# A hand-written task order on one core: all tasks in a new order, the first pair's operands loaded in another order, the four pieces of w_in issued together

## The chip, the core and the metric

The kernel runs on one core of a Trainium2 chip. The metric is the device time of one execution in microseconds, the median of several runs. The engines are named as in the profile: PE (matrix products; PEld is its weight load), DVE, ACT and POOL (vector work, activation functions, general work), SP (issues DMA transfers). Sixteen DMA engines move the data; transfers issued by SP go through the queue q1, those issued by POOL through q0.

## What is computed

A gated linear recurrence over the sequence feeds an MLP with a SiLU, token by token:

```python
B, H, S, D = 4, 8, 768, 48           # d_model = H * D = 384, d_ff = 2048
f = 1.0 / (1.0 + np.exp(-f_logit))
for t in range(S):
    state = f[:, :, t, :, None] * state + np.einsum('bhd,bhe->bhde', k[:, :, t], v[:, :, t])
    y[:, :, t] = np.einsum('bhd,bhde->bhe', q[:, :, t], state)
x = y.transpose(0, 2, 1, 3).reshape(B * S, H * D)     # 3072 tokens of 384
h = x @ w_in                                           # 384 -> 2048
return ((h * (1.0 / (1.0 + np.exp(-h)))) @ w_out).astype(np.float32)
```

Inputs and output are float32 in HBM; the products run in bfloat16.

## The kernel before

The sequence of each of the four batches is cut into six chunks of 128 tokens. Two chunks form a pair, and `PAIRS` lists twelve of them: pairs 0 to 3 (form T) are chunks 0 and 1 of one batch, whose tokens alternate over the partitions, so that one load of 384 KB has runs of 384 bytes; pairs 4 to 11 (form N) are the same chunk of two batches, with runs of 192 bytes. A pair goes through these tasks, each a word `kind.pair.half` in the text `PLAN`:

- `f`, `k`, `q`, `v`: loads of the pair's inputs (line 228), nearly all issued by SP.
- `E`, `L` (lines 234, 238, 241): exp(-f) and its logarithm ln(1 + .) on ACT, into `lf`. `cs` (lines 305 to 315): PE sums the logarithms along the chunk with triangular matrices (`triu`, `tincl`, `tstrict`); small products with `ones` or `halves` give the chunk's total decay.
- `ia`, `a` (line 317): exp(c) and exp(-c) of that sum c on ACT; `al` (lines 256, 319): the total decay.
- `ki`, `qg` (line 322): k times exp(c) and q times exp(-c), on DVE or POOL, into `qk`. `vb`: v cast to bfloat16 (line 182 on ACT, 184 on DVE and POOL).
- `tq`, `qkc` (lines 329, 184): `qk` transposed on PE and copied out of PSUM; or `qkD` (line 337): transposed by a DMA that SP issues.
- `sc` (lines 346, 350): scores k times q; `at` (line 354): the scores times a mask. `y`, `yi` (lines 263, 362, 366): scores times v, and q times the state of the chunk before. `d` (lines 275, 383): k times v, the chunk's share of the state; `sd`, `su` (lines 387, 393): the new state.
- `yc`, `yT`, `xc` or `yD`: y cast, transposed on PE and copied into `xT`, or transposed by a DMA.
- `mi.P.j` (line 249): six products of the MLP's first matrix, two 128-wide column blocks of h for all 256 tokens of a pair; `si` (line 254): SiLU on ACT into `hT`; `mo.P.i.n` (line 286): four products of the second matrix for one chunk; `oc`, `so`: the result copied from PSUM and stored.
- `wi.n`, `wo.n` (lines 207, 210): a quarter of w_in or w_out, read as float32 and written to SBUF as bfloat16 by a DMA that POOL issues. Piece n of w_in holds the columns of mi.P.2n and mi.P.2n+1.
- `idle.w.n` (line 436): n matrix products of w columns whose result nobody reads.

A word such as `wi.1:G:` or `qg.1.1:V:0` also names the engine (S for SP, A, V, G for POOL, P for PE) and the buffer of the class, numbered in `SLOTS`, that the task takes. The whole order is thus written out by hand or by a search outside the kernel: each engine works through its own tasks in the order of `PLAN`, strictly one after the other, and waits by semaphores for what a task reads and for the buffer that it takes. A load that takes a buffer waits, with all of SP's later work behind it, until the former content was read. `LAST` cuts the last output tile in two. Where ACT goes from SiLU to exponentials or back it loads a table (line 485); this happens 17 times in this order and in the new one.

Before the plan the kernel issues the first four loads, builds the triangular matrices, masks and the identity on POOL and DVE and clears some buffers.

## Time and profile before

| | us |
|---|---|
| median of 3 runs | 177.82 (177.65 to 178.28) |
| the profiled execution | 178.21 |
| its span, first to last instruction | 176.4 |
| PE busy | 169.9 (96%) |
| ACT busy | 130.1 (74%) |
| DVE busy | 82.2 (47%) |
| POOL busy | 61.6 (35%) |

The profiled execution's own time is 1.8 us longer than its span. Busy PE time counts matmuls from issue to modelled end, and they overlap: 576 products of 256 columns at a mean of 272 ns are busy for 69.2 us, since one is started about every 109 ns. A timeline row such as `1.37 4.45 PE ... x10` gives the start, the time from there to the end of the last one, and the count. The granted clock of PE was 1.00 throughout.

### The profile page before, as it was taken

What the parts mean: (1) busy time and instruction counts of PE and PEld (TensorE: products, weight loads), DVE (VectorE), ACT (ScalarE), POOL (GpSimd) and SP (SyncE); (2) the same over time, 40 slices, a digit from 0 to 9 for tenths busy, and PEclk for the clock granted to TensorE, in tenths of its full rate; (3) what the DMA queues carried; (4) which work ended last, traced back from release to release, by engine and by line L of the source; (5) the groups of instructions that cost most, each with busy time, mean ns of one, the idle gap of its engine ahead of it and who ended that gap; (6) DMA issues with size and microseconds to landing.
All of it is one profiled execution on the core that took longest, in us unless ns stands there. A gap on an engine that the chain in (4) does not pass through costs nothing.

```text
span 176.4 us, 4754 instructions
## 1 busy us (share of the span) xinstructions
PE 169.9 (96%) x1927; PEld 125.4 (71%) x1930; DVE 82.2 (47%) x166; ACT 130.1 (74%) x239; POOL 61.6 (35%) x104
## 2 busy tenths in 40 slices
PE   6988999999999999999999999999999999999992
PEld 2446688666886788766787686686697676786872
DVE  7189770047795784124777155035770152520101
ACT  3967578952999989999489687997699575191630
POOL 6059394002383348400646323400434880000000
PEclk9999999999999999999999999999999999999999
DMA  5999999989999999996598797899996999323202
GB/s 147 323 325 264 208 232 198 187 156 250 207 189 214 222 202 198 184 201 140 103 231 165 148 227 153 212 151 209 223 187 147 221 139 289 71 52 127 89 4 89
DMA packets 110677, 32.12 MB, mean 182 GB/s; under 512 B 104096, under 2 KB 110528, under 8 KB 110656
## 3 DMA queue, kind: packets, MB, share of 16 engines
...
q0 software_dynamic: 3936, 3.74, 11.9%
...
q8 instruction: 15, 0.25, 0.6%
...
## 4 chain that ended last, share of the span: by engine, by line
PE 72%; ACT 11%; DVE 5%; DMA 5%; issue 2%; SPq 2%; POOL 1%; DVEq 0%; POOLq 0%
PE pb L286 32%; PE pb L249 26%; DMA k<-in_k_dram 3%; ACT x L317 3%; ACT hT L254 3%; DVE qk L322 2%; PE pb L350 2%; ACT L485 2%; DMA f<-in_f_logit_dram 2%; PE pb L362 2%; PE pb L366 2%; PE pb L346 1%; PE pb L312 1%; DVE atm L354 1%; PE pb L374 1%
## 5 line engine op out<-in xcount | busy, mean ns | idle before, releaser
L249 PE MATMUL pb<-xT,w_in_sb 128*128 128x256 bf16 x576 | 69.2, 272 | 0.3 <-ACT hT L254 0.2
L286 PE MATMUL pb<-w_out_sb,hT 128*128 128x384 bf16 (+2 forms) x400 | 68.6, 320 | 0.3 <-DVE yb L184 0.3
L249 PEld LDWEIGHTS <-w_in_sb 128*128 128x128 bf16 x576 | 54.8, 98 | 9.1 <-issue 0.9
L254 ACT ACTIVATE hT<-pb 128x512 bf16<-128x512 f32 x96 | 50.5, 611 | 11.1 <-PE pb L249 10.9
L286 PEld LDWEIGHTS <-hT 128*128 128x128 bf16 x400 | 37.2, 98 | 20.8 <-issue 0.4
L393 POOL TENSOR_TENSOR st<-sd,al 48x192 bf16<-48x192 f32 x40 | 21.4, 535 | 58.5 <-PE pb L362 33.2
L317 ACT ACTIVATE x<-pb 128x384 f32<-128x384 f32 x48 | 21.1, 499 | 5.8 <-PE pb L305 3.3
L354 DVE TENSOR_TENSOR atm<-pb,triu 128x512 bf16<-128x512 f32 x32 | 20.1, 684 | 11.2 <-PE pb L350 6.6
L485 ACT ACT_TABLE_LOAD x17 | 21.8, 1283 | 0.3
L184 DVE COPY ob<-pb 128x384 f32<-128x384 f32 (+1 forms) x11 | 5.7, 528 | 26.3 <-PE pb L286 26.3
L322 POOL TENSOR_TENSOR qk<-k,x 128x384 bf16<-128x384 f32 x11 | 12.0, 1102 | 6.6 <-ACT x L317 2.2
L387 DVE TENSOR_TENSOR sd<-pb,st 128x384 f32<-128x384 f32 x16 | 8.8, 552 | 11.6 <-PE pb L383 10.1
L322 POOL TENSOR_TENSOR qk<-q,x 128x384 bf16<-128x384 f32 x11 | 11.1, 1012 | 8.7 <-DMA q<-in_q_dram 6.1
L234 ACT ACTIVATE e<-f 128x768 f32<-128x768 f32 x12 | 10.1, 839 | 4.4 <-DMA f<-in_f_logit_dram 4.4
L182 ACT COPY ob<-pb 128x384 f32<-128x384 f32 (+1 forms) x14 | 6.6, 474 | 7.6 <-PE pb L286 7.1
L322 DVE TENSOR_TENSOR qk<-q,x 128x384 bf16<-128x384 f32 x13 | 8.0, 633 | 7.7 <-ACT x L317 7.6
L354 DVE TENSOR_TENSOR atm<-pb,mask 128x512 bf16<-128x512 f32 x16 | 10.2, 684 | 2.1 <-PE pb L346 1.0
L436 PE MATMUL pb<-zero,triu 128*128 128x512 bf16 (+1 forms) x26 | 9.4, 465 | 1.4 <-POOL triu masks.py:66 1.4
L322 DVE TENSOR_TENSOR qk<-k,x 128x384 bf16<-128x384 f32 x13 | 9.1, 712 | 2.4 <-DMA k<-in_k_dram 2.1
L184 DVE CAST yb<-pb 128x384 bf16<-128x384 f32 x14 | 7.6, 554 | 5.1 <-PE pb L366 2.6
L184 DVE COPY qkTT<-pb 128x1024 bf16<-128x1024 bf16 x7 | 4.6, 682 | 10.8 <-PE pb L329 10.8
L184 POOL CAST vb<-v 128x384 bf16<-128x384 f32 x12 | 6.4, 541 | 8.8 <-DMA v<-in_v_dram 7.1
...
## 6 DMA issues: line engine op xcount, KB each, us to landing
f<-in_f_logit_dram SPq DMA_DIRECT2D x11, 384.0 KB, 5.5
k<-in_k_dram SPq DMA_DIRECT2D x10, 384.0 KB, 5.6
q<-in_q_dram SPq DMA_DIRECT2D x10, 384.0 KB, 5.2
v<-in_v_dram SPq DMA_DIRECT2D x10, 384.0 KB, 4.9
...
w_in_sb<-in_moe_w_in_dram POOLq DMA_DIRECT2D x4, 384.0 KB, 8.7
w_out_sb<-in_moe_w_out_dram POOLq DMA_DIRECT2D x4, 384.0 KB, 9.7
...
```

The lines of the kernel that those rows point to most:

```text
L184: ENG[eng].tensor_copy(dst, src)
L234: return nc.scalar.activation(e, at("f", P)[:, j * w:(j + 1) * w], AF.Exp, scale=-1.0)
L249: nc.tensor.matmul(h[:, i, cols], w_in_sb[:, kk, n * 128:(n + 1) * 128], at("xT", P)[:, kk, cols], start=(kk == 0), stop=(kk == KT - 1))
L254: return nc.scalar.activation(at("hT", P)[:, 2 * j:2 * j + 2, :], at("h", P, j).rearrange("p (n c) -> p n c", n=2), AF.Silu)
L286: nc.tensor.matmul(at("o" + key, P, i)[:, 0:cols.stop - cols.start], at("hT", P)[:, n, i * C:(i + 1) * C], w_out_sb[:, n, cols], start=(n ...
L317: nc.scalar.activation(at(kind, P, i).rearrange("p h d -> p (h d)"), at("cs", P, i)[:, 0:HD], AF.Exp, scale=1.0 if kind == "ia" else -1.0)
L322: ENG[eng].tensor_mul(at("qk", P, i)[:, j, :, 0:D], heads("qk"[j], P, i), at("ia" if j else "a", P, i))
L354: ENG[eng].tensor_mul(at("atm", P, i)[:, r], at(f"s{r}", P, i).rearrange("p (n c) -> p n c", c=C), mask[:, None, :].to_broadcast([C, NP, C]))
L387: nc.vector.tensor_add(at("sd", P, i), d_ps, prev_state(P, i))
L393: nc.gpsimd.tensor_mul(at("st", P, i)[lo:lo + D, :, r * D:(r + 1) * D], at("sd", P, i)[lo:lo + D, :, r * D:(r + 1) * D], al_of(P, i)[lo:lo ...
L436: nc.tensor.matmul(buf["pb", int(got)][:, 0:rest[0]], triu, zero[:, 0:rest[0]], start=True, stop=True, skip_group_check=True)
L485: nc.scalar.preload_act_table_set(turns[n])
```

## The change

`PLAN` is replaced as a whole: 867 words in place of 846. In counts, the tasks are the same but for these: the dummy products are 17 of 512 columns and 8 of 256, before 26 and 3; the small products of `cs` are a task of their own, `on`; the second transposed tile of pair 6 becomes one on PE (`tq.6.0`, `qkc.6.0`) in place of `qkD.6.0`; eleven `su` go from POOL to DVE, and some `vb`, `oc`, `yc`, `xc` and `qg` change engines; one store goes from SP to POOL. The buffers f, k, q and v become one class `inp` of 24, and exp(-f) is written over f, so the class e goes. Only the first two loads are issued ahead of the preparations; the making of the matrices and the identity is in the plan (`mk.0`, `mk.1`, `mk.2` on POOL, `mv` on DVE). The dummy products take their weights from `zero`, before from `triu`.

At the start, SP's order is f.1, f.0, v.1, k.1, q.1, f.2, k.0, q.0, v.0, q.2, k.2, v.2; before it was f.1, f.0, k.1, q.1, v.1, f.2, k.0, q.0, v.0, q.2, k.2, v.2. ACT takes ia.1.0 and ia.1.1 ahead of a.1.1 and a.1.0, before the other way round; DVE takes ki.1.0 and ki.1.1 ahead of qg.1.1 and qg.1.0. POOL's first tasks are mk.0, mk.1, vb.1.0, vb.1.1, mk.2, wi.1, wi.3, wi.0, wi.2, ki.0.1, qg.0.1, su.1.0, wo.0, vb.0.1, wo.1, wo.2, wo.3; before they were vb.1.0, wi.1, su.1.0, wi.3, ki.0.1, wi.0, vb.0.1, wi.2, su.0.0, wo.0, su.0.1, wo.1, qg.2.1, wo.2, wo.3. PE's order around the first MLP products is now y.1, yi.1.1, sc.0.0, sc.0.1, yT.1.0, yT.1.1, idle, mi.1.2, mi.1.3, d.0, y.0, mi.1.6, idle, yi.0.1, mi.1.7.

The core of the diff, with the first and last words of both plans:

```diff
-LAST = {(11, 0): (("", slice(0, 256)), ("2", slice(256, 384)))}
+LAST = {(11, 1): (("", slice(0, 256)), ("2", slice(256, 384)))}
-SLOTS = dict(f=4, k=6, q=6, v=6, e=2, lf=3, x=5, qk=5, vb=7, qkT=4, qkTT=2, atm=4, yb=3, xT=4, hT=4, sd=2, al=6, ob=6, pb=8, st0=1, st1=1, st2=1, st3=1)
+SLOTS = dict(inp=24, lf=3, x=5, qk=5, vb=7, qkT=4, qkTT=2, atm=4, yb=3, xT=4, hT=4, sd=2, al=6, ob=6, pb=8, st0=1, st1=1, st2=1, st3=1)
...
-f.1.0:S:0 f.1.1:A: E.1.0:A:0 L.1.0:A:0 idle.512.10::0 cs.1.1:P:0 f.0.0:S:1 E.0.0:A:1 k.1.0:S:0 L.0.0:A:1 idle.512.1::1 cs.1.0:P:1
-q.1.0:S:0 idle.512.2::2 cs.0.0:P:2 idle.256.1::3 cs.0.1:P:3 a.1.1:A:0 qg.1.1:V:0 a.1.0:A:1 ia.1.1:A:2 ki.1.1:V: idle.512.1::4 tq.1.1:P:4 ia.1.0:A:3
-ki.1.0:V:1 v.1.0:S:0 f.2.0:S:0 qg.1.0:V: idle.512.3::5 tq.1.0:P:1 vb.1.1:V:0 vb.1.0:G:1 d.1:P:5,6 qkc.1.1:V:0 qkc.1.0:V: idle.512.1::7 idle.256.1::7
-sc.1.0:P:1,4 at.1.0.0:V:0 ia.0.0:A:0 k.0.0:S:1 ki.0.0:V:0 at.1.0.1:V: idle.512.2::7 idle.256.1::7 sc.1.1:P:7,1 at.1.1.0:V:1 at.1.1.1:V: a.0.1:A:2
-ia.0.1:A:3 sd.1.0:A:0 wi.1:G: al.1:A:0 E.2.0:A:1 L.2.0:A:1 q.0.0:S:1 a.0.0:A:1 qg.0.0:V: idle.512.1::5 cs.2.0:P:0 cs.2.1:P:5 al.2:A:1 ia.2.1:A:0
-su.1.0:G:0 ia.2.0:A:4 al.0:A:2 a.2.0:A:1 qg.0.1:V:1 idle.512.2::2 y.1:P:1,7 tq.0.0:P:4 v.0.0:S:1 yc.1.0:V:0 a.2.1:A:2 qkc.0.0:A:1 sd.1.1:V:0 wi.3:G:
-ki.0.1:G: tq.0.1:P:3 qkc.0.1:V: yT.1.0:P:1 yi.1.1:P: yc.1.1:A:0 wi.0:G: idle.512.2::2 sc.0.1:P:3,4 vb.0.1:G:0 at.0.1.0:V:0 yT.1.1:P:7 xc.1.0:A:0
-sc.0.0:P:6,5 at.0.0.1:V:1 at.0.0.0:V: vb.0.0:A:1 wi.2:G: idle.512.1::2 d.0:P:3,1 xc.1.1:A: sd.0.0:A:1 su.0.0:G:0 mi.1.2:P:7 mi.1.3:P:3 at.0.1.1:V:
...
+f.1.0:S:0 f.1.1:A: E.1.0:A: L.1.0:A:0 mk.0:G: mk.1:G: mv.0:V: idle.512.10::0 cs.1.1:P:0 idle.256.1::1 cs.1.0:P:1 f.0.0:S:1 E.0.0:A: L.0.0:A:1
+idle.256.1::2 on.1:P: cs.0.1:P:2 cs.0.0:P:3 on.0:P: v.1.0:S:2 k.1.0:S:3 ia.1.0:A:0 ki.1.0:V:0 vb.1.0:G:0 ia.1.1:A:1 ki.1.1:V:1 a.1.1:A:2 a.1.0:A:3
+ia.0.1:A:0 vb.1.1:G:1 idle.512.1::4 idle.256.1::4 d.1:P:4,5 q.1.0:S:4 qg.1.1:V: mk.2:G: idle.256.1::6 tq.1.1:P:1 qg.1.0:V: qkc.1.1:V:0 tq.1.0:P:6
+qkc.1.0:V: idle.512.3::7 sc.1.1:P:6,1 a.0.0:A:1 a.0.1:A:2 ia.0.0:A:4 f.2.0:S:5 E.2.0:A: al.1:A:0 al.0:A:1 L.2.0:A:1 sc.1.0:P:2,0 cs.2.0:P:3 cs.2.1:P:7
+on.2:P: k.0.0:S:0 q.0.0:S:1 v.0.0:S:2 ki.0.0:V:0 wi.1:G: a.2.1:A:4 at.1.1.0:V:0 qg.0.0:V: wi.3:G: at.1.0.0:V:1 idle.256.1::6 tq.0.0:P:6 at.1.1.1:V:
+at.1.0.1:V: wi.0:G: wi.2:G: sd.1.0:A:0 ki.0.1:G:1 ia.2.0:A:1 qkc.0.0:A:1 ia.2.1:A:0 qg.0.1:G: idle.512.1::2 idle.256.1::2 tq.0.1:P:4 su.1.0:G:0
+idle.512.1::2 y.1:P:0,1 a.2.0:A:2 yi.1.1:P: yc.1.1:A:0 wo.0:G: qkc.0.1:V: sc.0.0:P:4,6 sc.0.1:P:3,2 vb.0.1:G:0 yc.1.0:V:1 at.0.0.0:V:0 yT.1.0:P:0
+xc.1.0:A:0 yT.1.1:P:1 xc.1.1:V: idle.512.1::4 idle.256.1::4 mi.1.2:P:1 mi.1.3:P:0 al.2:A:2 vb.0.0:A:1 d.0:P:7,4 at.0.1.1:V:1 at.0.1.0:V: at.0.0.1:V:
+y.0:P:6,3 sd.0.0:A:0 mi.1.6:P:2 su.0.0:V:0 sd.0.1:V:1 idle.256.1::7 yi.0.1:P: yc.0.0:A:0 sd.1.1:V:0 mi.1.7:P:6 q.2.0:S:4 yc.0.1:A:1 yT.0.0:P:4
+xc.0.0:V:1 k.2.0:S:3 si.1.3:A:0 su.0.1:V:0 wo.1:G: yT.0.1:P:3 mi.1.0:P:5 mi.1.1:P:4 si.1.2:A: xc.0.1:V: mi.0.2:P:3 mi.0.6:P:1 mi.0.3:P:0 mi.0.5:P:7
...
+mi.5.4:P:5 si.3.0:A: mo.3.0.0:P:6 si.3.7:A: si.3.5:A: si.3.3:A: mo.3.1.0:P:7 mo.3.1.1:P: mi.5.5:P:2 mo.3.1.2:P: tq.6.0:P:1 mo.3.1.3:P: oc.3.1:V:2
+mo.3.0.1:P: mo.3.0.2:P: vb.4.0:V:1 so.0.1:S: mi.5.7:P:7 qkc.6.0:V:1 k.4.0:S: si.5.1:A:0 si.5.4:A: ia.4.0:A:4 E.7.0:A: L.7.0:A:1 qkD.4.1:S:0 a.4.0:A:0
...
+so.8.1:G: so.10.0:S: si.11.1:A:0 mi.11.0:P:4 si.11.0:A: mi.11.3:P:0 mi.11.2:P:5 mi.11.5:P:4 si.11.2:A: mi.11.7:P:1 so.6.1:S: si.11.3:A: mo.11.0.0:P:5
+mo.11.0.1:P: si.11.5:A: mo.11.1.0:P:4,2 mo.11.1.1:P: si.11.4:A: mo.11.0.2:P: si.11.7:A: si.11.6:A: mo.11.0.3:P: oc.11.0:V:3 mo.11.1.2.0:P:
+mo.11.1.2.1:P: so.11.0:S: oc.11.1.0:A:1 so.11.1.0:A: oc.11.1.1:V:4 so.11.1.1:S:
...
-        if kind in ("wi", "wo"):
-            n, parts = rest[0], count[kind]
-            if kind == "wi":
-                w = d_ff // parts
-                nc.gpsimd.dma_start(out=w_in_sb[:, :, n * w:(n + 1) * w], in_=w_in_src[:, :, n * w:(n + 1) * w])
-            else:
-                w = NT // parts
-                nc.gpsimd.dma_start(out=w_out_sb[:, n * w:(n + 1) * w, :], in_=w_out_src[:, n * w:(n + 1) * w, :])
+        if kind == "wi":
+            cols = slice(512 * rest[0], 512 * (rest[0] + 1))
+            return nc.gpsimd.dma_start(out=w_in_sb[:, :, cols], in_=w_in_src[:, :, cols])
+        if kind == "wo":
+            rows = slice(4 * rest[0], 4 * (rest[0] + 1))
+            return nc.gpsimd.dma_start(out=w_out_sb[:, rows, :], in_=w_out_src[:, rows, :])
+        if kind == "mk":
+            if rest[0] == 2:
+                return make_identity(nc, ident)
+            return make_upper_triangular(nc, tstrict if rest[0] else triu, 1.0, diag=not rest[0])
+        if kind == "mv":
+            nc.vector.tensor_copy(tincl, triu)
+            for t in (tincl, tstrict):
+                nc.vector.memset(t[0:HC, HC:C], 0.0)
+            for r in range(2):
+                half = slice(r * HC, (r + 1) * HC)
+                for j in range(2):
+                    for t in range(2):
+                        nc.vector.tensor_copy(masks[j][half, t * HC:(t + 1) * HC], (tincl if j <= t else tstrict)[half, half])
...
-            e = at("e", P)[:, j * w:(j + 1) * w]
+            e = at("f", P)[:, j * w:(j + 1) * w]
             if kind == "E":
-                return nc.scalar.activation(e, at("f", P)[:, j * w:(j + 1) * w], AF.Exp, scale=-1.0)
+                return nc.scalar.activation(e, e, AF.Exp, scale=-1.0)
...
+        if kind == "on" and T:
+            lf, cs = at("lf", P), at("cs", P, 1)
+            for p in range(NP):
+                for j in range(2):
+                    nc.tensor.matmul(cs[:, HD + 2 * p:HD + 2 * p + 2], lf[:, j, 2 * p:2 * p + 2, :], halves,
+                                     start=False, stop=(j == 1), skip_group_check=True)
+            return
...
-                if i == 1:
-                    for p in range(NP):
-                        for j in range(2):
-                            nc.tensor.matmul(cs[:, HD + 2 * p:HD + 2 * p + 2], lf[:, j, 2 * p:2 * p + 2, :], halves,
-                                             start=False, stop=(j == 1), skip_group_check=True)
             else:
                 nc.tensor.matmul(main, triu, lf[:, i, :, 0:D], start=True, stop=True, skip_group_check=True)
-                if not last:
-                    for p in range(NP):
-                        nc.tensor.matmul(cs[:, HD + p:HD + p + 1], lf[:, i, 2 * p:2 * p + 2, :], ones, start=False, stop=True, skip_group_check=True)
+        elif kind == "on":
+            lf, cs = at("lf", P), at("cs", P, i)
+            for p in range(NP):
+                nc.tensor.matmul(cs[:, HD + p:HD + p + 1], lf[:, i, 2 * p:2 * p + 2, :], ones, start=False, stop=True, skip_group_check=True)
...
-                nc.gpsimd.tensor_mul(at("st", P, i)[lo:lo + D, :, r * D:(r + 1) * D], at("sd", P, i)[lo:lo + D, :, r * D:(r + 1) * D],
+                ENG[eng].tensor_mul(at("st", P, i)[lo:lo + D, :, r * D:(r + 1) * D], at("sd", P, i)[lo:lo + D, :, r * D:(r + 1) * D],
...
-                nc.tensor.matmul(buf["pb", int(got)][:, 0:rest[0]], triu, zero[:, 0:rest[0]], start=True, stop=True, skip_group_check=True)
+                nc.tensor.matmul(buf["pb", int(got)][:, 0:rest[0]], zero[:, 0:C], zero[:, 0:rest[0]], start=True, stop=True, skip_group_check=True)
...
-        loads = [t for t in plan if t[0] in SRC][:4]
-        for t in loads:
+        first = [t for t in plan if t[0] in SRC][:2]
+        first = [t for t in first if t[2] == "A" or t is first[0]]
+        for t in first:
             run(*t)
         nc.scalar.preload_act_table_set(TABLES["exp"])
-        make_upper_triangular(nc, triu, 1.0, diag=True)
         nc.vector.memset(zero, 0.0)
         nc.vector.memset(ones, 1.0)
         if two:
-            nc.gpsimd.memset(tincl, 0.0)
-            nc.gpsimd.memset(tstrict, 0.0)
-            for r in range(2):
-                half = slice(r * HC, (r + 1) * HC)
-                make_upper_triangular(nc, tincl[half, half], 1.0, diag=True)
-                make_upper_triangular(nc, tstrict[half, half], 1.0, diag=False)
             nc.vector.memset(halves, 0.0)
             for r in range(2):
                 nc.vector.memset(halves[r * HC:(r + 1) * HC, r:r + 1], 1.0)
         for cls in ("lf", "qk"):
             for s in range(SLOTS[cls]):
                 nc.vector.memset(buf[cls, s][:, :, :, D:64], 0.0)
-        make_identity(nc, ident)
         for b in range(B):
             nc.vector.memset(buf[f"st{b}", 0], 0.0)
-        if two:
-            for r in range(2):
-                half = slice(r * HC, (r + 1) * HC)
-                for j in range(2):
-                    for t in range(2):
-                        nc.vector.tensor_copy(masks[j][half, t * HC:(t + 1) * HC], (tincl if j <= t else tstrict)[half, half])
         for n, t in enumerate(plan):
             if n in turns:
                 nc.scalar.preload_act_table_set(turns[n])
-            if t not in loads:
+            if t not in first:
                 run(*t)
```

165 lines of the change are left out of this document (87 added, 78 removed).

## The prediction

> **What bounds the kernel now.** I read the page first: shares by engine, the forty slices and the costliest groups.
>
> ```profile
> span 176.4 us, 4754 instructions
> PE 169.9 (96%) x1927; PEld 125.4 (71%) x1930; DVE 82.2 (47%) x166; ACT 130.1 (74%) x239; POOL 61.6 (35%) x104
> PE   6988999999999999999999999999999999999992
> PEclk9999999999999999999999999999999999999999
> DMA  5999999989999999996598797899996999323202
> L249 PE MATMUL pb<-xT,w_in_sb 128*128 128x256 bf16 x576 | 69.2, 272 | 0.3 <-ACT hT L254 0.2
> L286 PE MATMUL pb<-w_out_sb,hT 128*128 128x384 bf16 (+2 forms) x400 | 68.6, 320 | 0.3 <-DVE yb L184 0.3
> L322 DVE TENSOR_TENSOR qk<-k,x 128x384 bf16<-128x384 f32 x13 | 9.1, 712 | 2.4 <-DMA k<-in_k_dram 2.1
> L322 DVE TENSOR_TENSOR qk<-q,x 128x384 bf16<-128x384 f32 x13 | 8.0, 633 | 7.7 <-ACT x L317 7.6
> ```
>
> TensorE is busy 96% of the span, and the two groups of the expert product wait only 0.3 us each. A new order can therefore win almost nothing in the long middle, but it can lose there. What is left is the start, where PE runs dummy matmuls while pairs 1 and 0 go through the recurrence. In the same slices the DMA row stands at 9: the loads are a second resource that is full. The chain of waits gives the start in order of time (start, duration, what).
>
> ```profile
> 7.54 1.15 ACT x L317 x3
> 8.71 1.34 DVE qk L322 x2
> 11.64 0.43 PE pb L436 x2
> 13.76 1.85 DVE atm L354 x3
> 17.41 0.68 DVE qkTT L184
> 18.14 0.42 PE pb L346 x16
> 19.50 0.45 PE pb L275 x16
> 19.94 1.42 PE pb L249 x12
> 21.36 0.51 PE pb L263 x32
> 36.20 0.89 PE pb L329 x16
> 168.72 4.59 PE pb L286 x40
> ```
>
> Up to 19.9 us the chain hops between ACT, DVE and PE; the first expert matmuls come at 19.94, y.0 ends at 21.87, and from there the chain is almost all PE up to 173.3. So my landmark is the end of y.0: what stands behind it is a row of PE work that only its own length sets. All times below are on the profiled execution (178.21 us, of which 176.4 is the span); the median of the three runs is 177.82, 0.39 less, and I take that off at the end.
>
> **The compute path of the new start.** f of pair 1, both exponentials and logarithms stand where they stood, so ACT comes to exp(c) at 7.54. New: ia.1.0 first, then ia.1.1, a.1.1, a.1.0. Three of them took 1.15, so ki.1.0 starts at 7.95, if k is there. For the loads I need five of SP's issues (k.1, q.1, q.0, v.0 and k.2), and from the DMA view, in the same order, their time from issue to landing, the last number of each row.
>
> ```profile
> 1.79 0.58 SPq L228 DMA_DIRECT2D k<-in_k_dram  x1
> 2.42 1.74 SPq L228 DMA_DIRECT2D q<-in_q_dram  x1
> 7.78 1.15 SPq L228 DMA_DIRECT2D q<-in_q_dram  x1
> 8.97 1.11 SPq L228 DMA_DIRECT2D v<-in_v_dram  x1
> 11.50 1.15 SPq L228 DMA_DIRECT2D k<-in_k_dram  x1
> ...
> k<-in_k_dram SPq DMA_DIRECT2D x1, 384.0 KB, 4.8
> q<-in_q_dram SPq DMA_DIRECT2D x1, 384.0 KB, 5.4
> q<-in_q_dram SPq DMA_DIRECT2D x1, 384.0 KB, 4.9
> v<-in_v_dram SPq DMA_DIRECT2D x1, 384.0 KB, 4.9
> k<-in_k_dram SPq DMA_DIRECT2D x1, 384.0 KB, 12.1
> ```
>
> SP's new order is f.1, f.0, v.1, k.1, q.1, f.2, k.0, q.0, v.0. v.1 takes k.1's place and lands at 1.79 + 4.8 = 6.6; k.1 takes q.1's and lands at 2.42 + 5.4 = 7.8, just ahead of its use at 7.95; q.1 takes v.1's, 9.0 (POOL's row below starts on it at 9.09). The places of q.0 (7.78 + 4.9 = 12.7) and v.0 (8.97 + 4.9 = 13.9) are unchanged.
>
> DVE then sets the pace: two ki 1.34, to 9.3; two qg of 0.63, to 10.55 (q has landed); two copies of 0.68, to 11.9 (the transposes, 0.89 for two tiles, lie between); ki.0.0 0.71, to 12.6; one mask product and qg.0.0, 0.68 + 0.63, to 13.9; three mask products 1.85, to 15.8. So y.1 can start at 15.8, against 15.67 before: the new order of q and k alone wins nothing there, because the old path had the same DVE work ahead of y.1. The gain comes behind it. qkc.0.1 is next on DVE, 16.5, and lets the scores of pair 0 start, against 18.14; yc.1.0 0.55, one mask product 0.68 and xc.1.1 0.36 bring mi.1.2 to 18.1, against 19.94; three more mask products 1.85 bring y.0 to 20.0 and its end to 20.5, against 21.87. That is 1.4 us won if no load is late. Of that I take 0.1 for the idle.256 (half of the 0.43 / 2 of a 512 one) that now stands behind y.0.
>
> Edits with one answer. The dummy matmuls are fewer (17 of 512 and 8 of 256, before 26 and 3), but they stand in waits, and the path above doesn't pass through them. tincl, the masks and ident move into the plan (mv, mk): POOL's mk.2 stands behind vb.1.1 and before the w_in pieces, and is needed only by the transposes at 9.9. E in place and one class of input buffers add no wait at the start: k.0, q.0 and v.0 take buffers that L.1, L.0 and vb.1.1 have left before SP comes to them. Eleven su move from POOL to DVE, which is 47% busy. qkD.6.0 becomes eight PE transposes: 0.89 / 2 = **+0.45 us** on PE, the resource that bounds the rest. The tail, one 384-wide and two cut products with their stores, keeps its form: nothing.
>
> **The w_in pieces.** This is where I expect the loss. Three views: POOL's timeline, and the packets that the two DMA queues started in 9.6 to 12.9, 15.6 to 17.2 (one row each) and 20 to 24 us (both rows).
>
> ```profile
> 3.34 0.21 POOL masks.py:197 MEMSET ident<- 128x128 bf16 x1
> 3.62 0.29 POOL masks.py:199 TENSOR_SCALAR_AFFINE_SELECT ident<-ident 128x128 bf16<-128x128 bf16 x1
> 9.09 0.55 POOL L184 CAST vb<-v 128x384 bf16<-128x384 f32 x1 [5.18 <-DMA v<-in_v_dram]
> 9.58 0.91 POOL L207 DMA_DIRECT2D w_in_sb<-in_moe_w_in_dram  x1
> 13.35 0.81 POOL L207 DMA_DIRECT2D w_in_sb<-in_moe_w_in_dram  x1
> ...
> q1 hardware_dynamic: 2837, 1.07, 117.1%
> q0 software_dynamic: 4, 0.00, 0.8%
> q0 software_dynamic: 589, 0.58, 86.0%
> q1 hardware_dynamic: 596, 0.23, 32.5%
> ```
>
> Before, w_in.1 was issued at 9.58, and until 12.9 only loads moved: 2837 packets in 3.3 us, 860 per us, 1.2 us for a load of 1024 packets (384 KB by 384 B). The second piece, issued at 13.35, had moved next to nothing by 17.2. So a piece starts 3.4 to 3.9 us after its issue. Once both queues move, they start the same number of packets, 589 and 596 in 4 us: a load gets 149 packets per us, a sixth of its rate. Before, v.0 was through (13.9) when the first piece came to speed, and the later pieces were spread by POOL's work between them.
>
> Now POOL has v.1 at 6.6, two casts of 0.55 and the identity's 0.21 + 0.29 to do, and issues the four pieces from 8.2 on in a row, 0.8 to 0.9 each. They flow from 11.6 to 12.1 on, without a break. q.0's last packets (it lands at 12.7, its data ends about 0.4 earlier, at 12.3) are touched little. v.0's 1024 packets come after that, at 149 per us: 6.9 us, to 19.2, landing 19.6. That is the low end. The high end is k.2 of before: issued at 11.50, with 12.1 to landing, 23.6; it had the queue at full rate in 15.6 to 17.2 and still landed 6.4 us after w_in.3 began, since a load has landed only with its last packet. v.0 has no such head start: the 1.6 us at full rate were worth more than a whole load, which at 149 packets per us would have taken 6.9. So the 6.4 us from 12.1, 18.5, are too short, and k.2's landing itself, 23.6, is too long, as it stood behind q.2; I set the high end at 22.2. I take **20.9**, the middle. Behind it: ACT's or POOL's cast 0.55, d.0 0.45, y.0 0.51, end 22.4 against 21.87, +0.55 us. PE can't pass d.0: the queue has mi.1.2 and mi.1.3 ahead of it (1.42, done by 19.6) and everything else behind; on ACT, sd.0.0, yc.0.0 and the first silu stand behind vb.0.0, on POOL the last three w_out pieces behind vb.0.1.
>
> Sum: 0.55 + 0.1 + 0.45 = +1.1 us. For the middle I add 0.3: the 0.3 us rows leave less than 1 us to win, and the longest such wait that I find in the chain,
>
> ```profile
> 106.06 0.32 issue
> ```
>
> 0.3 us after a row of transposes and a k load on SP, is what one misjudged landing costs; an order searched anew makes its own. 178.21 + 1.4 = 179.6; less 0.39: **179.2 us**.
>
> Weighed against the Trainium skill, "DMA: Bandwidth & Descriptors", Queues, rings and completion order: an engine goes round between the queues it has work for at packet granularity. That speaks against issuing the pieces in a row, and the trace's 589 against 596 bears it out. By that rule alone v.0 lands at my low end, 19.6, and the result would be 177.9.
>
> **Rivals.**
> *A, v.0 is in time.* If the pieces flow later or the loads keep their rate until v.0 is through, d.0 doesn't wait: -1.3 + 0.45 = -0.85 on the profile, **177.0**. For it: POOL must make descriptors for four pieces at once, which before it never did, and the second piece of before took 3.9 us, not 3.4. It decides from a landing before about 19.0. Against it: equal packets from 20 to 24.
> *B, my forecast*, v.0 between 19.6 and 22.
> *C, worse sharing.* q.0's tail is caught too and v.0 lands as late as k.2 did, 23.6: y.0 ends at 25.1, +3.2, with 0.55 **181.6**. PE would then stand still over 4 us. By "TensorE: Matmul & The Clock Gate", Part 1, an idle window of about 3.4 us halves the clock; no run here shows it, and it would add some 1.7 as an estimate from that page.
> *D, the middle goes wrong*: several landings on SP's queue are misjudged; four stalls of 0.3 above mine, **180.4**.
> *E, the pieces flow at once.* Then from 9.2 on f.2's end and k.0 crawl at 149 packets per us while the 4 x 384 w packets of 1 KB pass (10.4 us), k.0 lands near 20, q.0 at 21.3, y.1 starts at 23.8 instead of 15.8, y.0 ends at 28.5 instead of 20.5: +6.6, with 0.55 **185.0**. The rows above speak against it (3.4 us). In the skill's "DMA: Bandwidth & Descriptors", Latency and other measured facts, the first byte of a GpSimd transfer comes after about 1 us.
>
> **How the numbers follow.** Chances: A 0.25, B 0.45, C 0.14, D 0.13, E 0.03. B is likeliest, so 179.2; its own range is 177.9 to 180.4. Leaving out the best part of A, the end of C and E, the range is 176.8 to 182.0. Of this kernel, 0.3% is 0.53 us, about what a measurement can tell. Faster by more than that needs most of A (0.8 of it) and a little of B with a better middle: 0.25. Within: the rest of A, the low end of B (v.0 near 19.6 gives +0.1): 0.14. Slower: 0.61.
>
> **What would show it.** Right: v.0's time to landing over 10 us where it was 4.9; packets of both queues in equal number from about 12.5 to 20; a gap on PE before d.0 (L275's new line) released by vb, after mi.1.3; w_in.1 issued at 8.2; y.1 at about 15.8 and the first expert matmul about 18, both ahead of or level with before. Wrong: v.0 landing by 18 with y.0 done at 20.5 (A), mask products or copies of DVE as what PE waits for at d.0, stalls of PE over 0.5 us behind 25 us (D), or a first w packet before 11 us (E).

## The result: 189.17 us in place of 177.73, and the profile after

The changed kernel takes 189.17 us (median of 6 runs, 187.54 to 190.39), the kernel before 177.73 on the same chip (177.60 to 178.28): a ratio of 1.063, 95% interval 1.058 to 1.069. "Slower" was right; 179.2 was not, and the range ended at 182.0. The profiled execution is the quickest of the six, 187.54 with a span of 185.8, so the traces differ by 9.4 us and the medians by 11.4; what the other five runs lose beyond it no trace shows, but their granted clock is lower, 0.979 to 0.982 against 0.989. Here and below a median counts all runs, and a ratio leaves out those over 1.5% above the fastest of the same kernel.

The page of the changed kernel, rows as in the prediction (L266 and L310 are now the lines of mi and mo, the MLP's products, which the prediction calls expert matmuls):

```profile
span 185.8 us, 4770 instructions
PE 170.6 (92%) x1932; PEld 127.2 (68%) x1934; DVE 92.4 (50%) x192; ACT 130.3 (70%) x236; POOL 52.4 (28%) x79
PE   7683899999987999999996999999999999999993
PEclk9999799999999999999999999999999999999999
L266 PE MATMUL pb<-xT,w_in_sb 128*128 128x256 bf16 x576 | 69.8, 272 | 2.6 <-DVE xT L182 1.7
L310 PE MATMUL pb<-w_out_sb,hT 128*128 128x384 bf16 (+2 forms) x400 | 68.2, 320 | 0.0
```

PE is nearly as busy as before (170.6 us against 169.9): of the 9.4 us, 8.7 are standing still. The row by slices shows where: a hole in the fourth slice (14 to 19 us), a lower clock in the fifth, and dents in the 12th, 13th and 22nd.

**The start.** The chain of waits (start, length, what), then y.0 itself from PE's timeline:

```profile
8.00 8.30 DMA inp<-in_q_dram
16.39 0.57 DVE qk L347
17.01 0.62 PE pb L354 x8
22.59 1.47 PE pb L266 x12
24.06 0.49 PE pb L299 x16
...
24.34 0.56 PE L287 MATMUL pb<-vb,atm 64*128 64x48 bf16 x32
```

q.0, issued at 8.00, landed at 16.30 and not at 12.7. DVE waited for it, PE for DVE; y.0 ends at 24.90 against 21.87, **3.0 us late**. POOL's timeline, the DMA view of 12 to 16 us and v.0's rows show why:

```profile
8.23 3.21 POOL L211 DMA_DIRECT2D w_in_sb<-in_moe_w_in_dram  x4
...
q0 software_dynamic: 563, 0.56, 84.4%
q1 hardware_dynamic: 595, 0.22, 32.2%
...
9.18 1.06 SPq L245 DMA_DIRECT2D inp<-in_v_dram  x1
inp<-in_v_dram SPq DMA_DIRECT2D x3, 384.0 KB, 13.7
```

The row of four was issued from 8.23, as predicted, and from 12 to 16 us both queues started about the same number of packets, 595 of the loads in 4 us (149 packets per us, as predicted). v.0 landed at 9.18 + 13.7 = 22.9. The granted clock of PE, by stretches of the changed kernel (the column behind POOL's):

```profile
17.00:19.00 2.00, 1.99 (x18) 1.59 (x19) 1.75 (x3) 1.81 (x4) 1.93 (x4) 0.67 1.21 206
19.00:21.00 2.00, 1.64 (x51) 1.28 (x53) 1.25 (x2) 0.58 (x3) 0.60 (x1) 0.50 1.20 206
21.00:22.00 1.00, 0.98 (x38) 0.77 (x31) 0.63 (x1) 0.50 (x2) 0.00 (x0) 0.95 1.19 205
```

**The middle.** From y.0's end to the end of the span it was 154.5 us before and is 160.9: **6.4 us more**, twice the loss of the start. PE's waits behind 25 us (in total, times, longest), before and after:

```profile
PE pb L286 <- DVE yb L184: 0.3, 1, 0.3
PE pb L249 <- ACT hT L254: 0.2, 1, 0.2
```

```profile
PE pb L266 <- DVE xT L182: 1.7, 1, 1.7
PE pb L415 <- DVE vb L182: 1.0, 1, 1.0
PE pb L266 <- ACT ob L180: 0.7, 1, 0.7
PE pb L398 <- POOL vb L182: 0.6, 1, 0.6
PE pb L335 <- ACT x L340: 0.4, 1, 0.4
```

0.5 us in two waits has become 4.4 in five, on four different kinds of work. I also sum, over all products of PE, by how much the interval to the next one exceeds the median interval of its form, where that is over 0.1 us; I call this the stalls. Behind y.0 they are 2.7 us before and 8.2 after, which is 5.5 of the 6.4 us. The added products (eight transposes and a dummy) are 0.4, at the median interval of their form.

### The profile page after: what moved, and what is told of

It reads as the page before. It is cut to its first block, busy times and chain, and to the rows that moved or that the text cites. A ratio compares the mean times of both kernels' runs of the same rounds, so it can differ in the third digit from the quotient of the medians.

```text
span 185.8 us, 4770 instructions
## 1 busy us (share of the span) xinstructions
PE 170.6 (92%) x1932; PEld 127.2 (68%) x1934; DVE 92.4 (50%) x192; ACT 130.3 (70%) x236; POOL 52.4 (28%) x79
## 4 chain that ended last, share of the span: by engine, by line
PE 71%; DMA 9%; DVE 9%; ACT 5%; issue 3%; POOL 1%; SPq 0%; DVEq 0%; ACTq 0%
PE pb L310 31%; PE pb L266 26%; DMA inp<-in_q_dram 4%; DVE qk L347 3%; DMA inp<-in_v_dram 3%; DVE st L425 2%; PE pb L378 2%; DMA inp<-in_f_logit_dram 2%; PE pb L354 2%; PE pb L394 2%; PE pb L398 1%; PE pb L331 1%; PE pb L415 1%; ACT x L340 1%; POOL qk L347 1%
## 5 line engine op out<-in xcount | busy, mean ns | idle before, releaser
L266 PE MATMUL pb<-xT,w_in_sb 128*128 128x256 bf16 x576 | 69.8, 272 | 2.6 <-DVE xT L182 1.7
L310 PE MATMUL pb<-w_out_sb,hT 128*128 128x384 bf16 (+2 forms) x400 | 68.2, 320 | 0.0
L271 ACT ACTIVATE hT<-pb 128x512 bf16<-128x512 f32 x96 | 51.0, 603 | 18.1 <-PE pb L266 17.7
L266 PEld LDWEIGHTS <-w_in_sb 128*128 128x128 bf16 x576 | 54.8, 98 | 12.3 <-issue 4.0
L310 PEld LDWEIGHTS <-hT 128*128 128x128 bf16 x400 | 37.2, 98 | 20.6 <-ACT hT L271 0.2
L347 POOL TENSOR_TENSOR qk<-inp,x 128x384 bf16<-128x384 f32 x24 | 25.5, 1073 | 35.7 <-ACT x L340 18.8
L182 DVE COPY ob<-pb 128x384 f32<-128x384 f32 (+1 forms) x14 | 7.4, 536 | 38.5 <-PE pb L310 33.0
L347 DVE TENSOR_TENSOR qk<-inp,x 128x384 bf16<-128x384 f32 x24 | 15.8, 678 | 8.4 <-ACT x L340 4.7
L425 POOL TENSOR_TENSOR st<-sd,al 48x192 bf16<-48x192 f32 x18 | 9.4, 522 | 31.7 <-PE pb L394 14.9
L182 POOL CAST vb<-inp 128x384 bf16<-128x384 f32 x13 | 6.8, 531 | 34.2 <-DMA inp<-in_v_dram 34.2
L251 ACT ACTIVATE inp<-inp 128x768 f32<-128x768 f32 x12 | 10.1, 839 | 1.9 <-DMA inp<-in_f_logit_dram 1.8
L425 DVE TENSOR_TENSOR st<-sd,al 48x192 bf16<-48x192 f32 x22 | 10.8, 489 | 1.2 <-ACT sd L180 0.9
L180 ACT CAST yb<-pb 128x384 bf16<-128x384 f32 x13 | 6.3, 488 | 7.1 <-PE pb L398 4.6
L354 PE MATMUL pb<-ident,qk 128*128 128x128 bf16 x72 | 5.7, 230 | 3.5 <-DVE qk L347 3.4
L468 PE MATMUL pb<-zero 128*128 128x512 bf16 (+1 forms) x23 | 7.4, 428 | 1.4 <-DVE halves L494 1.2
```

Source lines behind the costliest of these rows:

```text
L180: nc.scalar.copy(dst, src)
L182: ENG[eng].tensor_copy(dst, src)
L251: return nc.scalar.activation(e, e, AF.Exp, scale=-1.0)
L266: nc.tensor.matmul(h[:, i, cols], w_in_sb[:, kk, n * 128:(n + 1) * 128], at("xT", P)[:, kk, cols], start=(kk == 0), stop=(kk == KT - 1))
L271: return nc.scalar.activation(at("hT", P)[:, 2 * j:2 * j + 2, :], at("h", P, j).rearrange("p (n c) -> p n c", n=2), AF.Silu)
L310: nc.tensor.matmul(at("o" + key, P, i)[:, 0:cols.stop - cols.start], at("hT", P)[:, n, i * C:(i + 1) * C], w_out_sb[:, n, cols], start=(n ...
```

## Experiments

Plan edits are given as words; "behind X" is the place in the plan. All ratios are to the kernel before on the same chip, with the 95% interval in brackets; the changed kernel's is 1.063 (1.058 to 1.069).

### The start: when the row is issued

```diff
# row late: the changed kernel; split: the same without moving wi.1
-wi.1:G: a.2.1:A:4 ... wi.3:G: ... wi.0:G: wi.2:G: sd.1.0:A:0 ki.0.1:G:1
+a.2.1:A:4 ... sd.1.0:A:0 ki.0.1:G:1 wi.1:G: wi.3:G: wi.0:G: wi.2:G:
# row in the kernel before
-wi.1:G: ... wi.3:G: ... wi.0:G: ... wi.2:G:
+wi.1:G: wi.3:G: wi.0:G: wi.2:G: ...
```

Row late: 

> The kernel after with one word moved: the four w_in pieces, still in a row, stand behind ki.0.1 on POOL, so they are issued at about 12.7 us instead of 8.2. If the pieces cost time because their packets share the DMA engines with q.0 and v.0 (start theory), q.0 lands at 12.7 instead of 16.3 and v.0 at 13.9 instead of 22.9, PE never turns cold, and mi.1.2 waits for w_in.1 alone (landing about 20.5); y.0 ends near 22.9 instead of 24.9: 2 us off 189.2, so 187, if the 6.4 us lost behind y.0 have causes of their own; 182 or less if those too come from loads that run late since the start. If the pieces are not the cause, q.0 and v.0 land as late as now and the time grows by about 4 us, since w_in comes later.

Split: 

> The kernel after with w_in.1 where it is (8.2 us) and the other three pieces behind ki.0.1 on POOL. Start theory: one piece of 384 packets shares from 11.2 to about 13.8, q.0 lands near 13.5, v.0 near 15.5, w_in.1 near 15; mi.1.2 goes at 18.5 to 19, y.0 ends near 21.3 instead of 24.9, so 185.6 with an independent middle, about 180 if the middle follows the start. If issuing in a row is harmless, no change (189).

Row in the kernel before: 

> The kernel before with w_in.3, w_in.0 and w_in.2 moved right behind w_in.1 on POOL (issue from 9.6 us on); nothing else. Start theory: what counts is what is still on the load queue when the pieces come to speed, at about 13; q.0 (12.7) and v.0 (13.9) are through, q.2 and k.2 have time until 24: 177.7, within 0.8. Rival, that a row costs in itself because the loads of pair 2 starve: 2 us or more slower.

Row late takes 188.55 us, 1.057 (1.050 to 1.064). q.0 and v.0 land 4.8 us after their issue, as in the kernel before, and yet no gain can be told: the issue of the four pieces fills POOL from 13.01 to 16.24, qg.0.1 stands behind it, and tq.0.1 with the whole PE queue waits until 17.33. The row's own 3.2 us became the new wait. Split takes 188.20, 1.055 (1.047 to 1.064): one early piece still holds q.0 to 15.3, d.0 starts 1.2 us earlier (22.75 against 23.99), and little of that reaches the end. The row in the kernel before, issued at 10.02, takes 177.75, 0.997 (0.993 to 1.002), no cost at all.

The other thing that the change names is the first pair. It was put into the old order alone, and then with the row:

```diff
-k.1.0 ... q.1.0 ... a.1.1 qg.1.1 a.1.0 ia.1.1 ki.1.1 ... tq.1.1 ia.1.0 ki.1.0 v.1.0 f.2.0 qg.1.0 ... tq.1.0 vb.1.1:V vb.1.0:G d.1
+v.1.0 k.1.0 ... q.1.0 ... ia.1.0 ki.1.0 vb.1.0:G ia.1.1 ki.1.1 vb.1.1:G a.1.1 a.1.0 qg.1.1 ... d.1 f.2.0 tq.1.1 qg.1.0 ... tq.1.0
# and, in the second kernel, wi.3 wi.0 wi.2 directly behind wi.1
```

First pair alone: 

> The kernel before with the change's first pair alone: SP issues v.1, k.1, q.1 in place of k.1, q.1, v.1; ACT takes ia.1.0, ia.1.1, a.1.1, a.1.0; DVE ki.1.0, ki.1.1, qg.1.1, qg.1.0; both vb of pair 1 on POOL and d.1 ahead of tq.1.1. Theory (the prediction's step: y.1 at 15.8 against 15.67, nothing gained or lost): y.1 within 0.3 us of before's, time within 0.5 us. Rival (q.1 last, landed at 9.0, holds tq.1.1 and all behind it, and the start sets the end): y.1 and the time 0.8 to 1.5 us later.

Both: 

> As the kernel before with the change's first pair, and the pieces of w_in in a row at wi.1's place as well, that is, both things that the change names, in the old order. Theory (the row is harmless where wi.1 is issued at 9.6, behind su's and vb's first tasks: 0.9974 by itself): within 0.6 us of before. Rival (vb.1.1, moved to POOL ahead of wi.1, or the loads' new order shift the row to before 9 us, and q.0 and v.0 are caught as in the changed kernel): q.0 later than 14, the clock down, 2 to 3 us slower.

The first pair alone takes 178.44, 1.001 (0.997 to 1.005); y.1 starts at 15.74 against 15.67. Both take **185.24, 1.041** (1.036 to 1.047). Two edits that each cost nothing cost 7 us together. The traces of the kernel with the row alone and of the one with both show it: POOL's row, and the packets from 12 to 16 us.

```profile
10.02 3.31 POOL L207 DMA_DIRECT2D w_in_sb<-in_moe_w_in_dram  x4
q0 software_dynamic: 474, 0.47, 70.7%
q1 hardware_dynamic: 1396, 0.52, 50.1%
```

```profile
7.67 3.23 POOL L207 DMA_DIRECT2D w_in_sb<-in_moe_w_in_dram  x4
q0 software_dynamic: 603, 0.59, 90.0%
q1 hardware_dynamic: 534, 0.21, 27.8%
21.22 1.03 DVE L322 TENSOR_TENSOR qk<-q,x 128x384 bf16<-128x384 f32 x2 [5.18 <-DMA q<-in_q_dram]
```

With v.1 loaded first, POOL is free 2.35 us sooner and issues the row at 7.67; its packets then run beside q.0's, and the loads start 534 packets in 4 us where they had started 1396. DVE waits 5.18 us for q.0, y.0 ends at 29.1, 7.2 us late, and the end is 7.0 late. With the first pair alone, w_in.1 is issued as early (7.60) but the other pieces come later: q.0 lands at 15.64, and nothing is lost. So it takes both, an early first piece and the row behind it.

How early decides how much. Where the row is issued 2.14 us after q.0 (row in the kernel before), q.0 lands at 12.75; 0.23 us after it (changed kernel) at 16.30; 0.23 us ahead of it (both) at 21.13. Ten profiles here, the changed kernel's and nine of those below, have the changed kernel's start, and q.0 lands in them between 16.15 and 21.23: the two latest, 19.29 and 21.23, are those in which the row was issued 0.08 us after q.0 and 0.19 us ahead of it.

The clock by itself: 16 dummies in the hole.

```diff
-idle.256.1::6 tq.0.0:P:6
+idle.512.16::6 tq.0.0:P:6
```

> The changed kernel with one edit: the dummy product of 256 columns ahead of tq.0.0 becomes 16 of 512 columns (about 213 ns each, 3.4 us), which fill the 3.43 us in which PE waited for q.0 from 13.58 to 17.01. Nothing else moves; q.0 lands as late. Theory (the wait also costs clock: granted 0.50 from 17 to about 21 after it): the granted clock stays near 1.0 between 16 and 22, y.0 ends near 23.5 in place of 24.87, and the time falls by 1.0 to 1.8 us, to 187.4 to 188.2 beside 189.17. Rival (from 17 on the waits for DVE and for v.0, landed at 22.9, set the times, the clock nothing): y.0 ends within 0.4 of 24.87, time within 0.4 us of the changed kernel's. Second rival (a chain of dummies that ends later than 17.01 delays tq.0.0): y.0 later than 25.

It takes 187.94 us (187.77 to 188.18), 1.055 (1.051 to 1.060); the granted clock is 1.00 in all four runs, where the changed kernel's six had 0.979 to 0.989. That is 1.2 us won on the median, inside the first theory's numbers, but the two intervals overlap a little, and in the profile y.0 ends only 0.4 earlier (24.50), since d.0 then waits 0.65 for the cast of v.0. The wide spread of the changed kernel's runs is gone too.

### The middle: repairing waits, moving su, loads

```diff
# six places: words moved (al.3 and al.6.0 get al buffers 6 and 7)
+ia.5.0 oc.0.1 ... qkc.3.1 su.1.1 ... xc.5.0 xc.5.1 su.5.1 ... xc.6.0 su.6.0 ... cs.8.0 on.8.0 ... q.11.0 v.10.0:S:8 ... mi.8.1 v.11.0:S:9
# spread (Q): qg.1.0:V: -> qg.1.0:G:, POOL: qg.1.0 wi.1 ki.0.1 wi.3 qg.0.1 su.1.0 wi.0 vb.0.1 wi.2 wo.0
# late (P):   POOL: ki.0.1 wi.1 qg.0.1 wi.3 su.1.0 vb.0.1 wi.0 wi.2 wo.0
```

Six places: 

> The changed kernel with the start untouched and six places behind 40 us reordered: oc.0.1 on ACT ahead of ia.3.1 (PE waited 0.88 us at 51.2 for its bank); su.1.1 on DVE moved behind qkc.3.1, out from ahead of qg.3.0, vb.3.1, qg.3.1, vb.5.0 (PE waited 1.16 at 56.0 for vb.5.0); su.5.1 behind xc.5.0 and xc.5.1 (0.72 at 71 to 73); su.6.0 behind xc.6.0 (1.86 at 98.9); on.8.0 right behind cs.8.0 (0.6 at 109.6); v.10.0 and v.11.0 issued earlier, into buffers of their own (0.76 at 152.9). For the first moves al.3 and al.6.0 get al buffers of their own. Theory (the middle's 6.4 us are six separate order mistakes, each a wait that PE cannot pass): of the 5.98 us of these stalls 4.5 to 6 go, time 183.2 to 184.7. Rival 1 (PE is behind because DVE has too much to do; a stall taken away comes back at the next wait): less than 2.5 us gained, time over 186.7. Rival 2 (only the longest, at 98.9, is real slack): about 1.5 to 1.9 gained, 187.3 to 187.7.

Six places and Q: 

> As the kernel with the six places reordered, and the pieces of w_in spread out again: qg.1.0 goes from DVE to POOL and POOL's order is vb.1.0, vb.1.1, mk.2, qg.1.0, wi.1, ki.0.1, wi.3, qg.0.1, su.1.0, wi.0, vb.0.1, wi.2, wo.0, so that wi.1 is issued at about 10.2 and not at 8.2, when q.0 and v.0 have had their packets for 2 us longer. Theory of the start (the early row costs q.0 and v.0 their share of the DMA engines): q.0 lands near 12.9, v.0 near 14.5, PE has no wait over 1 us ahead of tq.0.0 and keeps its clock, y.0 ends at 21.5 to 22.5 and the time is 2.3 to 3.3 us under that of the kernel with the middle alone (180 to 182). Rival (what is gained at the start is lost again before 40 us, at wo, v.2 or the first MLP): less than 1 us under it. Rival 2 (qg.1.0 on POOL beside qg.1.1 on DVE, both slow, delays pair 1): tq.1.0 over 0.8 us later, gain under 1.8.

Six places and P: 

> As the kernel with the six places reordered, but no piece of w_in ahead of ki.0.1: POOL's order is vb.1.0, vb.1.1, mk.2, ki.0.1, wi.1, qg.0.1, wi.3, su.1.0, vb.0.1, wi.0, wi.2, wo.0; qg.1.0 stays on DVE. Theory: q.0 and v.0 land 4.8 us after their issue (12.8 and 14.0), y.1 starts near 16, the clock stays up; wi.1, issued at about 13.1, flows from 16 and lands near 19.5, so mi.1.2 starts at 19.5 to 20 in place of 22.59; time 1.5 to 3 us under that of the kernel with the middle alone. Rival (the pieces now collide with q.2, k.2 and are each late for their mi): mi.1.2 after 21, or waits of mi for w_in_sb over 1 us in sum; gain under 1 us.

Six places alone takes 189.71, 1.063 (1.056 to 1.069): nothing was won. The waits for ob, x and POOL's vb are gone, that for xT fell from 1.7 to 0.3 and that for DVE's vb from 1.0 to 0.7, but others stand in their place. With Q it takes 185.41, 1.037 (1.029 to 1.045), and with P 186.41, 1.047 (1.041 to 1.053); in the profile of P the products mi wait three times for pieces of w_in, 2.4 us together, as its rival said. In the kernel with Q the start is fully repaired: no wait over 1 us up to y.0, granted clock 1.00 there, y.0's end at 21.6, before the old 21.87; and still 7.7 us are lost. PE's three longest waits behind 25 us in it:

```profile
PE pb L378 <- DMA qkT<-qk: 2.2, 1, 2.2
PE pb L331 <- DVE yb L182: 0.8, 1, 0.8
PE pb L415 <- DVE vb L182: 0.7, 1, 0.7
```

The first is for the second of the transposes of pair 10, and it costs more than its 2.2 us. PE stands from 145.56 to 147.71, and the granted clock is 0.50 from 148.6 to 152.0, when PE works again: 18 products mi take 3.51 us there, and 2.13 at 142.45. Of the four runs of this kernel the one with a clock of 0.997 took 183.33, the three with 0.987 to 0.991 took 185.0 to 186.1. So about 4 of the 7.7 us are this one wait (2.2, and some 1.7 as an estimate from 3.4 us at half the clock), and about 4 are left. The kernel with the six places alone has the same wait (1.9) and the same drop.

I first put this wait down to v.11.0, which the edit moved. The traces speak against it: v.11.0 stands behind both transposes of pair 10 on SP (PE waits for the one issued at 143.04 and landed at 147.66, v.11.0 was issued at 144.35), and in the kernel with all edits below, where it stands far ahead of them, the wait is 2.1 and the clock drops again. What the traces show is that PE comes to these scores 5.0 us earlier than in the changed kernel (145.16 against 150.18), while SP issues the transposes only 3.4 us earlier and the second takes 4.6 us to land in place of 3.2. So the changed kernel's other waits had hidden this one, and it came up when they were taken away, as rival 1 of the six places has it. What the six places are worth without it is not measured.

```diff
# su back: the changed kernel      # su in the kernel before, the same eleven
-su.0.0:V:0 ... (11 words)         -su.0.0:G:0 ... (11 words)
+su.0.0:G:0 ...                    +su.0.0:V:0 ...
# 24 load buffers: f, k, q, v take S:0 to S:23 in turn, before S:0 to S:7
# qk on DVE: the 22 words ki and qg with :G: behind q.2.0 become :V:
# all: Q, six places with v.11.0 behind v.10.0, su on POOL, 24 buffers
```

su back on POOL: 

> The kernel after with the eleven su that the change put on DVE back on POOL, at the same places of the order; nothing else. If the time lost behind y.0 is DVE's backlog (su between the products that PE waits for), the stalls near 51, 56 and 99 us go and 3 to 4 of the 6.4 us come back: 185 to 186. If it is late loads or the order in itself, within 1 us of 189.2. The start stays as it is (y.0 ends at 24.9 or up to 0.5 later, since su.0.0 then stands behind vb.0.1 on POOL).

su on DVE in the kernel before: 

> The kernel before, with the eleven su that the change gives to DVE (su.0.0, 0.1, 1.1, 5.1, 4.1, 4.0, 6.0, 6.1, 7.1, 9.1, 8.0) on DVE and nothing else moved. Theory (su on DVE is a cost by itself: 22 operations at 0.35 to 0.7 us ahead of work that PE waits for): PE's waits behind 25 us grow from 0.5 us to 1.5 to 3, time 1 to 2.5 us over before's. Rival (it costs only where the order leaves no slack, and the order of before does leave it): within 0.5 us of before.

24 buffers: 

> The changed kernel with one edit: its 48 loads take the 24 buffers of the class inp in turn, where its plan uses only 8 of them. SP's waits of loads for a buffer (19 us in sum between 25 and 150 us, by the changed kernel's waits) go. Theory (late loads are part of what the middle lost): v.10.0, q.8.0 and others land earlier, the wait of 0.76 at 152.9 goes and the time falls by 0.5 to 1.5 us. Rival 1 (the loads were in time, the waits come from DVE and ACT): within 0.4. Rival 2 (loads that run ahead take the DMA engines from w_in, w_out and the transposes): slower by 0.5 or more, PE waiting for w_in_sb, w_out_sb or qkT.

qk on DVE: 

> The changed kernel with all 22 ki and qg that POOL has behind q.2.0 given to DVE, so that DVE no longer multiplies float32 out of SBUF while POOL does (alone 0.56, 0.35 and 0.35 us for qk, st and vb; beside POOL 0.92, 0.69 and 1.15 in the changed kernel). Theory (the slowing of each by the other is most of what makes DVE late in the middle): qk and st on DVE return to 0.56 and 0.35, DVE busy 92.4 - 6.8 + 22 x 0.56 = 98 us, and PE's waits behind 25 us fall by 1 to 3 us. Rival (the amount of work in a strict order on DVE is what counts, not the speed of single operations): DVE with 98 us and 22 more tasks in its queue makes PE wait longer, time 1 to 4 us over the changed kernel's.

All: 

> The changed kernel with what helped or may help put together: pieces of w_in spread out and qg.1.0 on POOL (as in the kernel with both edits, 185.41), the six places reordered, v.11.0 directly behind v.10.0 ahead of the transposes of pair 10, all su on POOL, all 24 load buffers. If the parts add up: 185.4 less 1.5 to 2 for su and 1 to 2 for the wait of 2.3 us for the transposed pair 10: 181.5 to 183. Rival (waits move from place to place and the sum stays): 184.5 to 186. It stays slower than before in both.

su back on POOL takes 187.20, 1.047 (1.038 to 1.056), 2 us less, with a start that is 1 us later. But su on DVE in the kernel before takes 177.85, 1.000 (0.998 to 1.002): it is free there. The same work on the same engine costs time in one order and none in the other. With 24 buffers the ratio is 1.063 (1.060 to 1.067), from two of its four runs (188.7 and 189.5; the others took 193.0 and 194.6): nothing won; SP's waits for buffers were hidden. qk on DVE takes 192.47, 1.081 (1.078 to 1.084), 3 us worse, though each operation ran faster, as its theory had it (rows below). All together take 187.02, 1.052 (1.049 to 1.054), worse than Q and the six places alone: the parts don't add up, and the wait for the transposes of pair 10 stayed.

### The middle: which work feeds the waits

Four kernels on the one with the warm start (187.94) leave most of one kind of work out for pair 3 and later, with the order and all waits as they are.

```diff
# POOL less: tensor_mul of ki, qg on POOL
+n = 1 (of 8 heads) ... [:, j, 0:n, 0:D]
# DVE less: at
+n = 1 (of 4 blocks) ... [:, r, 0:n]
# ACT less: ia, a
+n = D (of HD) ... [:, 0:n]
# DMA less: unsplit loads of q, k, v
+src, dst = src[:, 0:1], dst[:, 0:1]     # form T; 0:2 in form N
```

> The kernel with the warm start (16 dummies ahead of tq.0.0, 187.94 us), in which POOL's ki and qg of pair 3 and later multiply one head of eight (128x48 in place of 128x384), so that each takes about 0.2 us in place of 1.0 and hardly runs beside DVE's; the rest of qk keeps an older content, so part of the product is left out. Orders, waits and all else stay. If the slowing of DVE and POOL by each other feeds the middle's waits: qk and st on DVE at 0.56 and 0.35, PE's stalls behind 30 us (8.3 by the issue intervals) fall by 2.5 to 4 us and the time with them. If it is DVE's amount of work or ACT: less than 1.

> The same base, in which DVE's masking (at) of pair 3 and later covers one block of four (128x128 in place of 128x512), about 0.25 us in place of 0.68, some 15 us less on DVE, with the rest of atm left at an older content: part of the masking is left out. If DVE's own work in its strict order feeds the middle's waits: 3 to 5 us gained. If the waits come from POOL beside it (the products of q and k, which this does not touch) or from ACT: less than 1.5.

> The same base, in which ACT's exponentials ia and a of pair 3 and later cover 48 columns of 384, about 0.2 us in place of 0.41 to 0.5, some 8 us less on ACT; the rest of the buffer keeps an older content, so part of the exponentials is left out. If ACT's phases of exponentials between two table loads feed the waits: 1.5 to 3 us gained. If not: less than 0.8.

> The same base, in which the 21 whole loads of q, k and v of pairs 3 and 6 to 11 bring one eighth of the data (48 KB in place of 384 KB); the rest keeps an older content, so part of the input is left out. If late loads and transposes feed the waits: 2 us or more gained, none of PE's waits on vb or qkT left. If the loads are hidden, as the kernel with 24 load buffers says (no gain): less than 1.

POOL less takes 185.63, 1.038 (1.031 to 1.045), against 1.055 (1.051 to 1.060) of the base: 2.3 us by the medians, 3 by the ratios. It is the only one whose interval lies clear of the base's. DVE less takes 188.09, 1.052 (1.044 to 1.060), not told apart from the base, though 13 us of DVE's work went (78.5 busy in place of 91.8). ACT less takes 188.20, 1.053 (1.046 to 1.060), not told apart either. DMA less takes 187.06, 1.046 (1.037 to 1.055), 0.9 us by the medians and 1.7 by the ratios, with intervals that overlap.

The profile with less POOL is of the slowest of its four runs: q.0 lands at 19.3 there and PE loses time at the start. Behind y.0 it is the quickest: from y.0's end to the end of the span it has 158.6 us, the base 161.5, DVE less 160.3, ACT less 161.5, DMA less 160.7. PE's waits for DVE's xT and vb are 0.3 each in it, where the base has 1.8 and 1.0.

Why POOL: two stretches of the changed kernel ahead of its longest wait, DVE's and POOL's rows.

```profile
95.51 0.56 DVE L347 TENSOR_TENSOR qk<-inp,x 128x384 bf16<-128x384 f32 x1
96.92 2.04 DVE L347 TENSOR_TENSOR qk<-inp,x 128x384 bf16<-128x384 f32 x2
98.88 1.51 DVE L425 TENSOR_TENSOR st<-sd,al 48x192 bf16<-48x192 f32 x2
100.42 0.36 DVE L182 COPY xT<-pb 128x384 bf16<-128x384 bf16 x1
...
96.77 1.00 POOL L347 TENSOR_TENSOR qk<-inp,x 128x384 bf16<-128x384 f32 x1
97.71 0.83 POOL L182 CAST vb<-inp 128x384 bf16<-128x384 f32 x1
98.51 1.30 POOL L347 TENSOR_TENSOR qk<-inp,x 128x384 bf16<-128x384 f32 x1
```

A product qk takes DVE 0.56 us while POOL does nothing, and 1.02 each while POOL multiplies and casts; st takes 0.75 in place of 0.35. The four together are 1.7 us longer so, and the copy xT behind them is what PE waits 1.7 us for. The groups by form in the changed kernel, and in the one with qk on DVE, where POOL has only two of the products qk left (the profile is of the slowest of its four runs):

```profile
L347 DVE TENSOR_TENSOR qk<-inp,x 128x384 bf16<-128x384 f32 x24 | 15.8, 678 | 8.4 <-ACT x L340 4.7 <-DMA inp<-in_q_dram 3.4
L425 DVE TENSOR_TENSOR st<-sd,al 48x192 bf16<-48x192 f32 x22 | 10.8, 489 | 1.2 <-ACT sd L180 0.9
```

```profile
L347 DVE TENSOR_TENSOR qk<-inp,x 128x384 bf16<-128x384 f32 x46 | 24.7, 559 | 14.7 <-DMA inp<-in_q_dram 7.3 <-ACT x L340 6.3 <-ACT lf L255 0.6
L425 DVE TENSOR_TENSOR st<-sd,al 48x192 bf16<-48x192 f32 x22 | 8.5, 387 | 1.2 <-ACT sd L180 0.9
```

678 ns falls to 559 and 489 to 387. So the slowing is real and comes from POOL. It is not new, though: in the kernel before, 13 of DVE's 26 products qk overlap with POOL's work for over 40% of their time and take 0.79 us on average, the other 13 take 0.55, and PE hardly waits. What the new order changed is what stands behind the slowed work. In POOL less, POOL's own operations are shorter as well (0.32 us in place of 1.07), and the run does not separate the two; that the waits which went were DVE's speaks for the slowing, without showing it.

## Why the prediction was wrong, by its steps

- **The compute path** held as far as it was seen with the loads in time: y.1 starts at 15.83 with P and at 15.74 with the first pair alone (15.8 predicted, no gain), and from there to y.0's end it is 4.8 us with Q (4.7 predicted, 6.2 before). No kernel here has both.
- **The pieces** held: issued at 8.23 (8.2), at speed by 12, about equal packets from 12 on, 149 of the loads' per us.
- **"q.0's last packets are touched little" failed**, and by the prediction's own numbers: with w_in flowing from 11.6 and q.0's data ending at 12.3, 0.7 us x 860 = 600 packets were left, and these at 149 per us take 4.0 us, with 0.4 to landing 16.0; it landed at 16.30. I had applied the slow rate to v.0 alone. v.0 stood behind it: 22.9, past my high end of 22.2.
- **The cold clock** was named beside rival C and left out of the sum: 1.2 us by the median of the warm kernel. The Trainium skill's page "TensorE: Matmul & The Clock Gate", Part 1, has the halving; the trace agrees (0.50 from 19 to 21 us).
- **y.0 at 22.4 (+0.55)** came at 24.90 (+3.0): rival C, which said 25.1.
- **The middle at 0.45 + 0.1 + 0.3** failed most: 6.4 us. The first two terms, the added products, were right (0.4); the 0.3 for new waits is the term that failed, with 5.5 us of stalls in its place. "An order searched anew makes its own" was rival D, right in kind, priced as four stalls of 0.3. The old order's 0.5 us of waits is no measure of what another order has. That su are on DVE "which is 47% busy" was the wrong argument: share of time says nothing of what stands behind a task in a strict queue, nor that DVE and POOL slow each other. The Trainium skill's page "SBUF — State Buffer", Who interferes with whom, says that a DVE instruction with two SBUF inputs contends with a GpSimd instruction that reads SBUF; I had not used it, and the rows above agree (0.56 against 1.02).
- C and D were priced as alternatives. Both came, and they add; but C's 181.6 with the middle's 0.3 and D's 1.2 is 183.1, so it is the size of D that leaves most of the miss.

What stays open: of the middle's 6.4 us, 2.3 to 3 go with POOL's products. su back on POOL is worth 2 us; whether these are the same is not tested. What goes with the loads, DVE's masking or ACT's exponentials can't be told from nothing. For some 3 us no single feeder was found. Repaired waits came back elsewhere, the longest at a transpose of pair 10 that PE now reached too early. No kernel here is faster than the one before beyond its interval; the nearest is the row in the old order, 0.997.
